# An attention and mixer kernel: halves of the first copies, the sixth pair's transposes, and the load of a small weight are moved

## The chip, the cores and the metric

The kernel runs on one core of a Trainium2 chip. The metric is device time in microseconds (us), the median of several executions. One more execution is profiled; its trace gives a start and a duration for every instruction. The engines are TensorE (PE for matmuls, PEld for its weight loads), VectorE (DVE), ScalarE (ACT), GpSimd (POOL) and SyncE (SP); a name with q is the queue of that engine from which it issues DMAs.

## What is computed

There are B = 8 batches of H = 8 heads, S = 576 tokens of D = 64 values, and 16 beacon keys and values ahead of the tokens. Causal attention gives x (8 x 576 x 512); a mixer of rank 32 along the tokens and a two-layer perceptron follow.

```
k_all = concat([beacon_k, k], axis=2); v_all = concat([beacon_v, v], axis=2)
scores = where(causal, -1e9, q @ k_all^T / sqrt(D))
a = softmax(scores)
x = (a @ v_all), heads side by side             # (B, S, 512)
u = x + (x^T @ U @ V)^T                         # U (576, 32), V (32, 576)
out = u + max(u @ w_ch1, 0) @ w_ch2             # w_ch1 (512, 2048), w_ch2 (2048, 512)
```

## The kernel before

**The tiles.** Attention runs by pairs of heads: a pair p is heads 2c and 2c + 1 of batch b, with b, c = divmod(p, 4), so pairs 0 to 3 are batch 0 and the sixth pair is p = 5. The layers run by blocks of 512 tokens over all batches. Banks of PSUM come from one ring of eight (`pst`), so the ninth tile waits until the first is read.

**One pair.** `qkT_units` (line 284) turns q and k: for each of the two, `one` makes 6 or 12 transposes on TensorE into one bank, and a copy moves them to qT or kT. For the first pair alone the copy is shared by ACT and DVE (line 623): `one` gives each half of the six token positions j, and as token 6p + j stands in column 6p + j, both halves write every column group. `score_units` (line 303) makes the products of keys and queries in four groups; visit 0 takes groups 0 and 1, visit 1 takes groups 2 and 3, or each alone ("two" and "three"). ACT's exponentials follow each visit; in pairs 0 to 4 the causal mask is added in PSUM by TensorE, in later ones DVE applies it to the exponentials. `av_unit` (line 353) makes a head's product with v, and DVE divides by the sum (lines 365 and 366) into xb.

**The mixing.** `mix_units` (line 370): `head` multiplies a batch's xb by Usb into qtp, which DVE copies to qts; `begin` and `most` add x, transposed by TensorE, and the product of qts with Vsb in four banks, which ACT and DVE in turn copy to uT ("settle", lines 402 to 408); `end` does so for the last 80 tokens with Vend, all on DVE.

**The layers.** `mlp_units` (line 442) gives 16 units `g_unit` (four matmuls with one 128-column slice of w1, then the rectifier on ACT or DVE) and 16 units `c_unit` (with w2). `feed` puts a block's units into a queue; `fill(n)` runs the next n. `FIRST` (line 653) says how many a slot p of the first eight runs between its attention steps. Block 0 needs uT of the first 512 tokens; its units 0 to 3 read w1's first quarter, 4 to 7 the second, and so on.

**The order.** All engines run what the program writes, in its order (line 699). In the first eight slots p (line 744), the steps of a slot are a list `seq`: the transposes of pair p + 2 (q, then k), a regroup of pair p + 3 from p = 4 on, visit 1 of the scores of pair p + 1, masks, the two products of pair p, and visit 0 of the scores of pair p + 2. Slot 3 is rewritten (line 767), as the first mixing is in it: products of pair 3, `cast_end`, transposes of pair 5, `head`, group two, `begin`, group three, `most`, `end`, visit 0 of pair 5. Four empty entries are then put ahead of block 0's units in the queue (line 780).

**The loads.** Most loads are issued by POOL, in order, each on one of a few semaphores, so a further load waits until an earlier one has landed. U and V are loaded by SP in `small_loads` (line 152) in float32: a marker that DVE writes holds the three loads of U and, behind them, the four copies of V until DVE has come that far. Then `cast` makes Usb and Vsb on POOL, and `cast_end` makes Vend on DVE. `load_rest` (line 731) calls them in slot 1 behind its second step; behind the cast, POOL issues the rest of v of batch 1, the last three quarters of w1, w2, and all later batches.

`keep_warm` (line 236) runs idle products of 512 columns on TensorE: eight at the start, two ahead of pair 0's scores, one ahead of pair 1's.

Of the kernel before, what the change touches and what calls it, by code (L numbers as in the profile page):

```python
# [11 lines left out]
F32 = mybir.dt.float32  # L12
# [6 lines left out]
P = 128  # L19
# [11 lines left out]
def kernel(  # L31
# [13 lines left out]
    nc = tc.nc  # L45
    B, H, S, D = q.shape
# [55 lines left out]
    def pst(shape, dtype, name):  # L102
        return psum.tile(shape, dtype, tag="ps", name=name)
# [48 lines left out]
    def small_loads():  # L152

        f = utp.tile([P, NT * R + S], F32, name="small", tag="ut")
        nc.vector.memset(f[:, 0:1], 0.0)
        uf, vf = f[:, 0 : NT * R].rearrange("p (j r) -> p j r", r=R), f[:, NT * R :]
        nc.sync.dma_start(out=uf[: nq[0], 0, :], in_=moe_U[0 : nq[0], :])
        nc.sync.dma_start(
            out=uf[:, 1 : NT - 1, :], in_=moe_U[q0[1] : QM, :].rearrange("(j p) r -> p j r", p=P)
        )  # L160
        nc.sync.dma_start(out=uf[:NL, NT - 1, :], in_=moe_U[QM:S, :])
        for cc in range(NCC):
            nc.sync.dma_start(out=vf[ds(R * cc, R), :], in_=moe_V)

        def cast():
            for rr, jj in ((nq[0], slice(0, 1)), (P, slice(1, NT - 1)), (NL, slice(NT - 1, NT))):
                nc.gpsimd.tensor_copy(out=Usb[:rr, jj, :], in_=uf[:rr, jj, :])
            nc.gpsimd.tensor_copy(out=Vsb, in_=vf[:, 0:QM])

        def cast_end():  # L170
            for cc in range(NCC):
                rs = ds(R * cc, R)
                nc.vector.tensor_copy(out=Vend[rs, cc, :], in_=vf[rs, QM:S])

        return cast, cast_end

    def emit_w1(i):
        w1r = moe_w_ch1.rearrange("(cc p) f -> p cc f", p=P)
# [105 lines left out]
    def qkT_units(turns, qT, kT, c, copies=((nc.vector.tensor_copy,), (nc.vector.tensor_copy,))):  # L284

        def one(i, dst, b0):
            ps = pst([P, SK], F16, name="tps")
            for j in range(TJ):
                n = TP + b0 if j == TJ - 1 else TP
                turns[i](ps, TP * j, n, j)  # L290
            w = TJ // len(copies[i])
            for a, copy in enumerate(copies[i]):
                js = slice(w * a, w * (a + 1))
                copy(  # L294
                    out=dst[:, c, b0 : b0 + S].rearrange("x (p j) -> x p j", j=TJ)[:, :, js],
                    in_=ps[:, 0:S].rearrange("x (j p) -> x p j", j=TJ)[:, :, js],
                )
            if b0:
                copies[i][-1](out=dst[:, c, 0:b0], in_=ps[:, S : S + b0])

        return [lambda: one(1, qT, 0), lambda: one(0, kT, Nb)]
# [348 lines left out]
    LAG = 10  # L650
    HINT = 5

    FIRST = [0, 0, 0, 0, 7, 5, 4, 4]

    QUOTA = {2: 4}

    IDLE = [8, 2, 1, 0]
    queue = []
    state = {"t": 0}

# [38 lines left out]
    with tc.manual_schedule(engines={ENG.PE, ENG.Activation, ENG.DVE, ENG.SP, ENG.Pool}):  # L699
        load_first()  # L700
        build_masks()
        for src, dst in zip((k[0], q[0]), Ls[0][0]):
            token_load(nc.gpsimd, src, dst, HALVES[1])
        v_beacon(beacon_v[0], vss[0])
        v_tokens(v[0], vss[0], HALVES[0])
        prs[0][0] = regroup(first, 0, 0, V, act_copy, beacons=False)
        keep_warm(pst([P, 512], F32, name="idle"), IDLE[0], plain)
        t0, sc = qkT_of(0), scores_of(0)
        for u in t0:
            u()  # L710
        sc[0](IDLE[1])
        masks = sc[2]
        prs[1] = [None, regroup(first, 1, 1, V)]
        for u in qkT_of(1)[::-1]:
            u()
        clear()
        sc[1]()
        sc = scores_of(1)
        sc[0](IDLE[2])

        Ls[1] = qk_tiles()
        (kt, qt), _ = Ls[1]
        token_load(nc.gpsimd, k[1], kt, HALVES[0])
        token_load(nc.gpsimd, q[1], qt, HALVES[0])
        key_beacons(nc.gpsimd, beacon_k[1], kt, ALLH)
        v_tokens(v[0], vss[0], HALVES[1])
        token_load(nc.gpsimd, k[1], kt, HALVES[1])
        token_load(nc.gpsimd, q[1], qt, HALVES[1])
        emit_w1(0)

        def load_rest():
            cast, cast_end = small_loads()
            cast()
            v_beacon(beacon_v[1], vss[1])
            v_tokens(v[1], vss[1], HALVES[0])
            emit_w1(1)
            v_tokens(v[1], vss[1], HALVES[1])
            emit_w1(2)
            emit_w1(3)
            emit_w2()  # L740
            return cast_end

        NP1 = NF * NH2
        for p in range(NP1):
            b, c = divmod(p, NH2)
            if c == 0 and NF <= b + 1:
                load_batch(b + 1)
            seq = []
            prior = masks
            if p + 2 < NP1:  # L750
                seq += [lambda i=i, p=p: qkT_of(p + 2)[i]() for i in range(2)]
            if NH2 + 3 <= p + 3 < NP1:
                seq.append(lambda p=p: regroup_of(p + 3))
            if p + 1 < NP1:
                one_by_one = sc[3]
                seq.append(sc[1])
                masks = sc[2]
            seq += [prior] + av_of(p)
            sc = []
            if p + 2 < NP1:  # L760
                new_qT_of(p + 2)
                sc = scores_of(p + 2)
                seq.append(lambda sc=sc, p=p: sc[0](IDLE[3] if p < NH2 else 0))
            if p == NH2 - 1:
                two, three = one_by_one
                _, head, (most, end), begin = mix_units(xbs[b], 0, False)
                seq = (
                    seq[-3:-1] + [cast_end] + seq[0:2] + [head, two, lambda: begin([0, 1]), three, most, end] + seq[-1:]
                )
            done = 0  # L770
            for i, u in enumerate(seq):
                u()
                if p == 1 and i == 1:
                    cast_end = load_rest()
                want = FIRST[p] * (i + 1) // len(seq)
                fill(want - done)
                done = want
            if c == NH2 - 1:
                if b == 0:
                    queue.extend([None] * 4)  # L780
                    feed(b)
                else:
                    mix(b)

        fill(AHEAD - 8)
        regroup_of(NP1)
        regroup_of(NP1 + 1)
        fill(8)
        t0, sc, t1 = qkT_of(NP1), scores_of(NP1), qkT_of(NP1 + 1)
        for u in t0 + sc[0:1] + t1[0:1] + sc[1:3] + t1[1:2]:  # L790
            u()
            fill(1)
        regroup_of(NP1 + 2)
        tr = []
        for p in range(NP1, NP):
            b, c = divmod(p, NH2)
            if c == 0 and b + 1 < B:
                load_batch(b + 1)
            if c == (2 if b + 2 == DT0 else 1) and DT0 <= b + 2 < B:
                load_whole(b + 2)  # L800
            if c == 0 and b + 1 == DT0:
                tr = turns(b + 1)
            if c == NH2 - 1 and DT0 < b + 2 < B:
                tr = turns(b + 2)
            sc = scores_of(p + 1) if p + 1 < NP else []
            qk = qkT_of(p + 2) if p + 2 < min(NP, DT0 * NH2) else []
            av = av_of(p)
            if c == NH2 - 1 or c == 0 and b + 1 == DT0:
                fill_turns(tr, NT)
            if c == 0 and b > NF:  # L810
                mix(b - 1)
            if c == (1 if b + 1 == DT0 else 0):
                fill_turns(tr, NT)
            seq = sc[0:1] + av[0:1] + qk[0:1] + sc[1:3] + qk[1:2] + av[1:2]
            if p + 3 < min(NP, DT0 * NH2):
                seq.append(lambda p=p: regroup_of(p + 3))
            quota = QUOTA.get(b, 9)
            done = 0
            for i, u in enumerate(seq):
                u()  # L820
                want = quota * (i + 1) // len(seq)
                fill(want - done)
                done = want
        mix(B - 1)
        guard()


        queue.insert(len(queue) - 22, guard_sum)
        fill(len(queue) - 12)
        n_bad = nc.values_load(badi[0:1, 0:1], min_val=0, max_val=P)  # L830
        fill(len(queue) - HINT)
        with tc.block():
            tc.mark_branch_hint_location("general", engines=[ENG.PE, ENG.Activation, ENG.DVE, ENG.SP, ENG.Pool])
            fill(len(queue))
# [95 lines left out]
```

## Time and profile before

| what | value |
|---|---|
| median of 3 runs | 360.03 us (359.12 to 363.38) |
| the profiled execution | 359.74 us |
| its span, first to last instruction | 358.1 us |
| mean granted TensorE clock | 0.990 |
| TensorE matmul busy | 350.0 us in 3134 instructions |
| VectorE busy | 188.5 us |
| ScalarE busy | 166.4 us |
| GpSimd busy | 96.3 us |

The views used are these. A row of the windows gives the stretch in us, its length, then the busy time of PE, PEld, DVE, ACT and POOL, each with its count of instructions, then the granted TensorE clock as a share of the full one, the busy share of the DMA engines, and GB/s. A row of the timeline gives the start in us, the duration in us, engine, line, operation, the tiles as out<-in, the shape and the count; in square brackets stands the idle time of the engine just before it and what ended it ("issue" where nothing that the profile shows ended it). A row of several instructions covers all of them, and its last matmul's tail overlaps what follows. A row of the chain of waits gives a start, a duration, and the work that the chain ran through; a DMA there lasts from its issue to its landing.

### The profile page before, as it was taken

How to read it: one execution, taken by the hardware profiler on the slowest of the kernel's cores; microseconds unless marked ns; L12 is line 12 of the kernel's file. 1: busy time of each engine (PE TensorE's matmuls, PEld its weight loads, DVE VectorE, ACT ScalarE, POOL GpSimd, SP SyncE). 2: the span in 40 equal slices, each digit the busy share in tenths (PEclk: the TensorE clock that was granted, in tenths of full speed). 3: DMA queues.
4: the chain of work that ended last, by engine and by line, in shares of the span. 5: the costliest groups of instructions: out<-in, count | busy, mean ns of one | idle time of the engine just before them, and what ended most of it. 6: DMA issues, size and time to landing. Idle time of an engine off the chain costs nothing.

```text
span 358.1 us, 7829 instructions
## 1 busy us (share of the span) xinstructions
PE 350.0 (98%) x3134; PEld 175.2 (49%) x3134; DVE 188.5 (53%) x488; ACT 166.4 (46%) x356; POOL 96.3 (27%) x135
## 2 busy tenths in 40 slices
PE   8989999999999999999999999999999999999995
PEld 3665455455565444444444444444454444444443
DVE  4667754588986454563455447445745522313311
ACT  4976761469646364367444654556503202401400
POOL 8729711609139027403730400000000000000000
PEclk9996999999999999999999999999999999999999
DMA  8998999999999949997999794142013215114111
GB/s 172 143 174 78 174 208 188 195 179 136 121 84 138 190 102 111 148 206 102 135 141 203 122 121 105 60 101 55 31 60 95 60 59 95 25 59 89 31 60 63
DMA packets 143946, 41.37 MB, mean 116 GB/s; under 512 B 128800, under 2 KB 139296, under 8 KB 143904
## 3 DMA queue, kind: packets, MB, share of 16 engines
q0 software_dynamic: 87408, 18.18, 67.4%
q1 hardware_dynamic: 56272, 22.34, 32.6%
q8 instruction: 26, 0.43, 0.5%
q10 hardware_dynamic: 224, 0.30, 0.2%
q14 instruction: 16, 0.13, 0.1%
HBM read 37.59 MB, written 9.44 MB: 131 GB/s over the span
## 4 chain that ended last, share of the span: by engine, by line
PE 81%; DMA 10%; DVE 3%; POOL 2%; SPq 1%; ACT 1%; issue 1%; ACTq 0%; POOLq 0%
PE cps L477 32%; PE gps L461 31%; PE sps L330 7%; PE po L357 6%; DMA st<-in_beacon_k_dram 6%; DMA w<-in_moe_w_ch_dram 2%; DMA small<-in_moe_V_dram 2%; PE tps L261 1%; DMA stk<-in_k_dram 1%; POOL vs L209 1%; PE cph L502 1%; ACT expt L336 1%; PE qtp L386 1%; DVE pr L254 1%; PE ups L422 1%; DVE uT L404 1%
## 5 line engine op out<-in xcount | busy, mean ns | idle before, releaser
L336 ACT ACTIVATE expt<-sps 128x496 f16<-128x496 f32 (+2 forms) x256 | 111.5, 532 | 63.0 <-PE sps L330 62.7
L461 PE MATMUL gps<-uT,w 128*128 128x512 f16 x576 | 135.5, 380 | 0.0
L477 PE MATMUL cps<-w,gT 128*128 128x512 f16 x560 | 132.7, 380 | 0.0
L465 ACT ACTIVATE gT<-gps 128x512 f16<-128x512 f32 x86 | 51.9, 607 | 95.8 <-PE gps L461 95.8
L461 PEld LDWEIGHTS <-w 128*128 128x128 f16 x576 | 52.1, 98 | 59.4 <-issue 3.4
L477 PEld LDWEIGHTS <-gT 128*128 128x128 f16 x560 | 49.8, 97 | 59.2 <-issue 6.8
L467 DVE TENSOR_SCALAR gT<-gps 128x512 f16<-128x512 f32 x58 | 40.0, 690 | 47.8 <-PE gps L461 46.7
L490 DVE TENSOR_TENSOR ob<-cps,ut 128x512 f32<-128x512 f32 x31 | 21.4, 690 | 49.6 <-PE cps L477 49.2
L357 PEld LDWEIGHTS <-expt 128*128 128x128 f16 (+1 forms) x960 | 36.8, 98 | 15.2 <-issue 1.9
L209 POOL DMA_DIRECT2D vs<-in_v_dram x50 | 39.5, 807 | 15.4 <-PE po L357 4.8
L357 PE MATMUL po<-vs,expt 128*128 128x65 f16 (+1 forms) x960 | 39.6, 195 | 0.2 <-DVE ob L490 0.2
L330 PE MATMUL sps<-qT,kT 64*128 64x80 f16 (+4 forms) x384 | 35.4, 290 | 0.1
L366 DVE TENSOR_TENSOR xb<-po,rec 128x320 f16<-128x320 f32 x64 | 31.5, 492 | 2.2
L307 DVE TENSOR_TENSOR expt<-expt,bigmask 128x512 f16<-128x512 f16 x54 | 22.6, 419 | 11.7 <-ACT expt L336 11.7
L365 DVE RECIPROCAL rec<-po 128x5 f32<-128x5 f32 x64 | 12.0, 187 | 23.2 <-PE po L357 23.2
L330 PEld LDWEIGHTS <-kT 64*128 64x128 f16 x384 | 11.8, 95 | 23.3 <-issue 15.3
L191 POOL DMA_DIRECT2D vs<-in_beacon_v_dram x8 | 4.3, 532 | 59.3 <-PE po L357 59.3
L560 POOL DMA_DIRECT2D st<-in_q_dram x20 | 16.9, 865 | 3.7 <-DMA vs<-in_v_dram 3.0
L560 POOL DMA_DIRECT2D st<-in_k_dram x20 | 16.9, 870 | 1.9 <-DMA vs<-in_v_dram 1.8
L404 DVE TENSOR_TENSOR uT<-ups,uT 128x496 f16<-128x496 f32 x20 | 12.1, 667 | 6.8 <-PE ups L422 3.6
L294 DVE COPY qT<-tps 128x576 f16<-128x576 f16 (+1 forms) x16 | 11.8, 736 | 5.1 <-PE tps L261 2.4
L294 DVE COPY kT<-tps 128x576 f16<-128x576 f16 (+1 forms) x16 | 11.7, 733 | 1.7 <-PE tps L267 1.1
(84 smaller groups left out, 145.6 us busy)
## 6 DMA issues: line engine op xcount, KB each, us to landing
out_dram<-ob SPq DMA_DIRECT2D x35, 256.0 KB, 2.2
vs<-in_v_dram POOLq DMA_DIRECT2D x18, 128.0 KB, 8.4
w<-in_moe_w_ch_dram POOLq DMA_DIRECT2D x4, 512.0 KB, 8.7
w<-in_moe_w_ch_dram POOLq DMA_DIRECT2D x2, 1024.0 KB, 14.5
st<-in_k_dram POOLq DMA_DIRECT2D x12, 128.0 KB, 7.4
st<-in_q_dram POOLq DMA_DIRECT2D x12, 128.0 KB, 9.3
st<-in_k_dram POOLq DMA_DIRECT2D x2, 576.0 KB, 13.1
st<-in_q_dram POOLq DMA_DIRECT2D x2, 576.0 KB, 16.1
```

The lines of the kernel that those rows point to most:

```text
L209: nc.gpsimd.dma_start(out=dst[a : a + nq[j], j, :, :], in_=src[hs, ds(q0[j], nq[j]), :].rearrange("h p d -> p h d"))
L294: copy(out=dst[:, c, b0 : b0 + S].rearrange("x (p j) -> x p j", j=TJ)[:, :, js], in_=ps[:, 0:S].rearrange("x (j p) -> x p j", j=TJ)[:, :, js],
L307: nc.vector.tensor_tensor(out=e4, in0=e4, in1=bigmask, op=ALU.min)
L330: nc.tensor.matmul(ps[g, i][:, ds(o, w)], kT[hp, c, ds(P * ch, P)], qT[hp, c, ds(qa, w)], start=not early, stop=True, skip_group_check=early,)
L336: nc.scalar.activation(out=ex[i][:, ds(SLOT * g, gw[g])], in_=ps[g, i][:, 0 : gw[g]], func=AF.Exp, scale=scale)
L357: nc.tensor.matmul(po[:, j, :], ex[0 : nk[c], ds(blk[(c, j)], P)], vs[0 : nk[c], ds(c * H * E + h * E, E)], start=(c == 0), stop=(c == j),)
L366: nc.vector.tensor_tensor(out=xb[:, :, ds(h * D, D)], in0=po[:, :, 0:D], in1=r.broadcast_to([P, NT, D]), op=ALU.mult)
L461: nc.tensor.matmul(g[:, 0:n], w1[:, cc, ts(dc, P)], uT[:, cc, ds(t0, n)], start=(cc == 0), stop=(cc == NCC - 1))
L465: nc.scalar.activation(out=gT["t"][:, dc, 0:n], in_=g[:, 0:n], func=AF.Relu)
L467: nc.vector.tensor_scalar_max(out=gT["t"][:, dc, 0:n], in0=g[:, 0:n], scalar1=0.0)
L477: nc.tensor.matmul(ps[:m, :], gT["t"][:, dc, ds(P * i, m)], w2[:, dc, :], start=(dc == 0), stop=turned and dc == NDC - 1, skip_group_check ...
L560: nc.gpsimd.dma_start(out=dst[a : m[j], j, :, :], in_=src[:, ds(q0[j], nq[j]), :].rearrange("h p d -> p h d"))
```

## The change

There are five edits.

1. In `qkT_units`, a copy that is shared is split by tokens: each engine takes half of the token groups p, with all six j, so it writes one half of the columns in a piece. Where one engine copies, nothing changes.
2. `small_loads` becomes a generator in three steps. U is loaded in slot 0 behind its second step (before: slot 1, second step). V, with a marker of its own, and the rest of `load_rest` follow at the end of slot 0.
3. Slot 3 is reordered: `head` and the mixing come right behind the products of pair 3, and the transposes of pair 5 behind `end`. Behind them block 0 is put into the queue and two of its units are run, and then comes visit 0 of pair 5. The four empty entries are gone.
4. `FIRST` for slots 4 to 7 goes from 7, 5, 4, 4 to 4, 4, 3, 3. With the two units of slot 3, and without the four empty entries, both kernels run 16 units of block 0 by the end of slot 7.
5. One idle product on a bank of its own is put between the transposes of q and of k of pair 0.

```
     def small_loads():
...
         nc.sync.dma_start(out=uf[:NL, NT - 1, :], in_=moe_U[QM:S, :])
+        yield
+        nc.vector.memset(vf[:, 0:1], 0.0)
         for cc in range(NCC):
             nc.sync.dma_start(out=vf[ds(R * cc, R), :], in_=moe_V)
...
-        return cast, cast_end
+        yield cast, cast_end
...
-            w = TJ // len(copies[i])
+            w = TP // len(copies[i])
             for a, copy in enumerate(copies[i]):
-                js = slice(w * a, w * (a + 1))
+                part = slice(w * a, w * (a + 1))
                 copy(
-                    out=dst[:, c, b0 : b0 + S].rearrange("x (p j) -> x p j", j=TJ)[:, :, js],
-                    in_=ps[:, 0:S].rearrange("x (j p) -> x p j", j=TJ)[:, :, js],
+                    out=dst[:, c, ds(b0 + TJ * w * a, TJ * w)].rearrange("x (p j) -> x p j", j=TJ),
+                    in_=ps[:, 0:S].rearrange("x (j p) -> x p j", j=TJ)[:, part, :],
                 )
...
-    FIRST = [0, 0, 0, 0, 7, 5, 4, 4]
+    FIRST = [0, 0, 0, 0, 4, 4, 3, 3]
...
-    IDLE = [8, 2, 1, 0]
+    IDLE = [8, 2, 1, 0, 1]
...
-        for u in t0:
-            u()
+        t0[0]()
+        keep_warm(pst([P, 512], F32, name="idle"), IDLE[4])
+        t0[1]()
...
         def load_rest():
-            cast, cast_end = small_loads()
+            cast, cast_end = next(loads)
             cast()
...
             if p == NH2 - 1:
...
+                def layers():
+                    feed(0)
+                    fill(2)
+
                 seq = (
-                    seq[-3:-1] + [cast_end] + seq[0:2] + [head, two, lambda: begin([0, 1]), three, most, end] + seq[-1:]
+                    seq[-3:-1] + [cast_end, head, two, lambda: begin([0, 1]), three, most, end]
+                    + seq[0:2] + [layers] + seq[-1:]
                 )
...
                 u()
-                if p == 1 and i == 1:
+                if p == 0 and i == 1:
+                    loads = small_loads()
+                    next(loads)
+                if p == 0 and i == len(seq) - 1:
                     cast_end = load_rest()
...
             if c == NH2 - 1:
-                if b == 0:
-                    queue.extend([None] * 4)
-                    feed(b)
-                else:
+                if b > 0:
                     mix(b)
```

## Prediction

> **What bounds the kernel now.** I read the page's busy times first, then windows of five microseconds and of one, then the timeline of the stretches that the change touches, and last the chain of waits for the landings of the loads.
>
> ```profile
> PE 350.0 (98%) x3134; PEld 175.2 (49%) x3134; DVE 188.5 (53%) x488; ACT 166.4 (46%) x356; POOL 96.3 (27%) x135
> ```
>
> ```profile
> 20.00:25.00 5.00, 3.92 (x97) 2.94 (x96) 3.48 (x11) 4.21 (x10) 0.67 (x3) 1.00 1.20 201
> 25.00:30.00 5.00, 4.22 (x65) 2.73 (x66) 2.67 (x9) 1.88 (x5) 3.22 (x6) 0.73 0.52 70
> 30.00:35.00 5.00, 5.00 (x66) 3.05 (x64) 4.36 (x11) 4.31 (x10) 5.00 (x8) 0.59 1.11 91
> 27.00:28.00 1.00, 0.29 (x3) 0.10 (x2) 1.00 (x2) 0.48 (x2) 1.00 (x3) 0.65 0.07 12
> ```
>
> TensorE is busy in 350.0 of 358.1 us, so 8.1 us is all that its idle time can give. Behind 35 us the windows show next to no gap, so a microsecond won ahead of it stays won unless a load is late. The stretch from 20 to 35 us is where this change works, and three things go wrong there at once. TensorE idles 1.08 + 0.78 us (windows one and two), its granted clock is 0.73 and 0.59 (half from about 27.3 on, since (0.27 + 0.41) x 5 / 0.5 = 6.8 us at half clock), and the DMA engines fall to a share of 0.07 at 27 us. The two idles are in these rows:
>
> ```profile
> 17.52 0.06 DVE L155 MEMSET small<- 128x1 f32 x1
> 18.98 2.56 SPq L163 DMA_DIRECT2D small<-in_moe_V_dram  x4
> 22.29 1.09 PE L357 MATMUL po<-vs,expt 128*128 128x65 f16 x30
> 23.81 0.49 DVE L366 TENSOR_TENSOR xb<-po,rec 128x320 f16<-128x320 f32 x1
> 25.00 0.32 PE L267 MATMUL tps<-ident,st 96*64 96x96 f16 x5 [1.08 <-issue]
> 25.25 0.47 PE L386 MATMUL qtp<-xb,Usb 112*32 112x128 f16 x20
> 25.65 0.36 PE L322 MATMUL sps<-negmask,identb 128*128 128x128 bf16 x4
> 26.26 0.61 PE L397 MATMUL ups<-ident,xb 112*128 112x112 f16 x8
> 26.71 0.22 PE L322 MATMUL sps<-negmask,identb 128*128 128x128 bf16 x1
> 26.80 0.60 POOL L168 CAST Vsb<-small 128x496 f16<-128x496 f32 x1 [1.78 <-DMA small<-in_moe_V_dram]
> 27.71 0.26 PE L322 MATMUL sps<-negmask,identb 128*128 128x128 bf16 x1 [0.78 <-DVE qT L294]
> 28.20 1.01 PE L397 MATMUL ups<-ident,xb 112*128 112x112 f16 x8
> 29.79 1.26 DVE L406 CAST uT<-ups 128x496 f16<-128x496 f32 x2 [1.20 <-PE ups L422]
> 30.31 0.98 PE L330 MATMUL sps<-qT,kT 64*128 64x496 f16 x4
> 30.96 0.48 DVE L406 CAST uT<-uend 128x320 f16<-128x320 f32 x1
> ```
>
> V is issued on SP from 18.98 us, and its last part holds the cast of Vsb on POOL until 26.80; the casts of Vend on DVE wait for the same parts. Behind Vend, in DVE's order, wait the copies of the sixth pair, whose bank the 0.78 us stall waits for; behind Vsb, in POOL's order, wait all later loads. The 1.08 us stall carries no releaser.
>
> **The change, part by part.** *U and V sooner.* V's start moves from behind the DVE work of slot 1 to behind that of slot 0, whose last product is here:
>
> ```profile
> 15.36 0.49 DVE L366 TENSOR_TENSOR xb<-po,rec 128x320 f16<-128x320 f32 x1
> 20.48 6.17 DMA small<-in_moe_V_dram
> 31.42 7.25 DMA w<-in_moe_w_ch_dram
> 39.56 1.04 PE L461 MATMUL gps<-uT,w 128*128 128x512 f16 x4
> ```
>
> The product ends at 15.85; one more marker (0.06, on an idle DVE) lets SP issue V at 15.93 in place of 18.98, 3.05 us sooner. U goes out after slot 0's copies, ahead of V, so it no longer delays V by its three issues. No compute waits behind SP's queue here. POOL's order does not change: it stands at the cast anyway, and everything behind the cast moves with V. Thus the second quarter of w1, which lands at 31.42 + 7.25 = 38.67, should land at about 35.6. Bounds for this shift: 0 if V only queues longer behind the loads of batches 0 and 1, and 4.0 if its 6.17 us also shrink by a microsecond in a shorter queue. I take 3.05, because every later load follows V's issue and the empty DMA stretch at 27 us can take them.
>
> [...]
>
> *Slot 3 reordered.* TensorE reaches the head of the first mixing right behind the two attention products (22.29 + 1.09 = 23.38), so the 24 transposes no longer cover DVE's last product, which ends at 23.81 + 0.49 = 24.30: a new wait of about 0.85 us, in place of the 1.08 and the 0.78. Behind it, at full clock: head 0.40 (25.25 to 25.65), group two 0.61 (to 26.26), first half of the mixing 0.45 (to 26.71), group three about 0.3, and 2.11 us of half-clock work (28.20 to 30.31), about 1.05 at full clock. That ends at 27.1. The 24 transposes take 0.64 (15.59 to 16.23 below), with a 0.2 us wait for a bank of the mixing that ACT empties: 27.95.
>
> ```profile
> 11.55 0.58 PE L330 MATMUL sps<-qT,kT 64*128 64x496 f16 x4
> 15.59 0.71 PE L267 MATMUL tps<-ident,st 96*64 96x96 f16 x24
> 16.23 0.63 PE L322 MATMUL sps<-negmask,identb 128*128 128x128 bf16 x6
> 31.23 1.18 PE L267 MATMUL tps<-ident,st 96*64 96x96 f16 x24
> 80.41 0.87 PE gps L461 x4
> 77.99 0.46 PE po L357 x15
> 39.15 0.48 PE L330 MATMUL sps<-qT,kT 64*128 64x336 f16 x8
> 37.66 0.69 PE L261 MATMUL tps<-ident,pr 96*128 96x96 f16 x12
> ```
>
> *Two layer units ahead of the scores.* The first unit reads all of uT, so it waits for DVE's settling, 1.26 + 0.48 = 1.74 us from about 26.95: it starts at 28.7, a wait of 0.75. Two units of 0.87 end at 30.45 and cover the copies to qT and kT, which DVE finishes at about 30.3. The scores (0.5) end at 31.0, where before they ended at 31.23 with no unit done. If that cover were gone, the scores would wait 1.6 us for the copies.
>
> From 31.0 the new order is transposes 0.64, unit 0.87, scores 0.41 (39.15 to the unit at 39.56), unit 0.87, product 0.46, with about 0.4 of waiting for ACT's exponentials: the fifth unit is reached at 34.65. It is the first that reads w1's second quarter, so it waits until 35.6: a new stall of 0.95 (bounds: 0, and 4.0 if the quarter lands at 38.67 as before). Before, that unit stood at 39.56, 0.9 us behind its quarter. To be where the kernel before was at 39.56, the new order still owes a product 0.46, scores 0.51 (0.58 without the tail of 0.07), transposes 0.55 (0.69 without a tail of 0.14) and scores 0.41, together 1.93: it is there at 35.65 + 1.93 = 37.6, a gain of 1.95.
>
> *The new quota (4, 4, 3, 3).* The same 16 units are run before slot 8 in both. In slots 6 and 7 one unit less stands between attention steps, and one instead of two (1.73 us) between the last product and the next head. That head needs DVE's 0.19 + 0.49 us; one unit of 0.87 just covers it. Bounds 0 to 0.5; I take 0.2 lost.
>
> *First copies by tokens, and the idle product.*
>
> ```profile
> 5.92 0.48 DVE L294 COPY qT<-tps 128x288 f16<-128x288 f16 x1 [0.39 <-ACT qT L597]
> 5.59 0.66 PE L261 MATMUL tps<-ident,pr 96*128 96x96 f16 x6 [0.32 <-DVE pr L254]
> 6.33 1.03 PE L241 MATMUL sps<-ident 128*128 128x512 f16 x2
> 6.97 0.48 DVE L294 COPY kT<-tps 128x288 f16<-128x288 f16 x1 [0.57 <-ACT kT L597]
> 7.69 0.98 PE L330 MATMUL sps<-qT,kT 64*128 64x496 f16 x4
> 10.77 13.44 ACT L336 ACTIVATE expt<-sps 128x496 f16<-128x496 f32 x32 [0.49 <-PE sps L330]
> ```
>
> DVE's half waits 0.39 and 0.57 us for ACT's half, since interleaved halves span the same bytes; halves by tokens do not. The keys are whole 0.5 us sooner, but TensorE reaches its scores only 0.1 us before now, held by its idle and mask products. The idle product (0.43 to 0.5) fits in the 0.32 us wait, so it costs 0.1 at most; it could end the slow start sooner (0.98 at 7.69 against 0.58 at 11.55 for the same four products). Together -0.1 to 0.6. What they win reaches slot 3 only through the gapless run of 32 exponentials up to 24.21, and by then the slots also wait for tokens that POOL loads, which do not move. I take 0.
>
> **The sum.** 1.95 - 0.2 = 1.75 us. The profiled execution took 359.74 (span 358.1), 0.29 under the median of the runs, 360.03. 359.74 - 1.75 = 357.99, so 358.0. The next load that could take the gain back is batch 2's, due at 42.82 + 20.49 = 63.31 with transposes at 64.32:
>
> ```profile
> 42.82 20.49 DMA st<-in_beacon_k_dram
> 64.32 0.42 PE L261 MATMUL tps<-ident,pr 96*128 96x96 f16 x6
> ```
>
> It moves with V, by 3.05, so 1.75 passes; if it moved by less than about 1.5, it would be late next.
>
> **The rivals.** *The weights are not sooner (slower).* If w1's second quarter lands at 38.67 as before, the fifth unit starts at 38.7 and the state of 39.56 is reached at 40.65: 1.1 us lost and the quota's 0.2, so 361.0. It decides from a landing at 37.4, a shift under 1.3 us. For it: the DMA share of 1.20 while V is under way. Against: the DMA engines are nearly empty at 27 us. Chance 0.13.
>
> *The clock is halved again.* TensorE idles 0.85 and 0.75 us in the same stretch, less than 1.08 + 0.78 but not by much. With half clock from 27.3 for the 6.8 us of before, two units take 3.46, scores 0.98 and transposes 1.18: 34.3 us from 28.7; then 2.6 at full clock to the fifth unit, 36.9, which no longer waits; state at 38.85, gain 0.7 less 0.2: 359.2. Chance 0.16. [...]
>
> *The weights are in time.* If the quarter lands by 34.65, the 0.95 us stall is gone: 357.0. It needs V to land a microsecond faster than 6.17. For it: V then no longer contends with w1's first quarter. Against: no row shows a shorter queue at 16 us. Chance 0.18.
>
> **Chances.** Forecast (357.3 to 358.8) 0.49, weights in time 0.18, clock 0.16, weights late 0.13, anything else 0.04. From 356.0 to 360.8 lie the forecast, the clock, most of the early weights with up to a microsecond more, and rather over half of the late ones, so about 0.88. The forecast's own range is 357.3 to 358.8. All cases lie inside 2% of 360.03 (352.8 to 367.2), which is about what a measurement of this kernel tells from no change: faster 0.02, same 0.96, slower 0.02.
>
> **What would show it.** In the changed profile: V issued near 16 us and the Vsb cast near 23.7; no DVE wait on ACT at the first copies; the head waiting for DVE's product; the first unit at about 28.7 and behind it the scores without a wait; the fifth unit behind a wait for a DMA near 35.6; a granted clock of 1.00 from 25 to 35 us. I am wrong if the Vsb cast is not two microseconds sooner, if a clock under 0.8 remains, or if a wait over half a microsecond appears behind 40 us.

## The result, and the profile after

The changed kernel took 358.49 us in the median of 22 runs, the kernel before 360.39 in 22 runs beside them. The ratio is 0.9948, with a 95% interval of 0.9929 to 0.9968: 1.9 us faster, well inside 2%.

The execution profiled with that result fell in a slower state that some executions show (363.27 us), so the profile after is that of another execution of the same kernel, `full_again`, which took 359.49 us with a span of 357.7. That is 1.0 us above the median, and why is told below. First the page's busy times, then its windows; the columns are as before.

```profile
PE 347.8 (97%) x3135; PEld 174.2 (49%) x3135; DVE 188.8 (53%) x489; ACT 165.9 (46%) x356; POOL 96.3 (27%) x135
```

```profile
20.00:25.00 5.00, 3.66 (x52) 2.32 (x52) 2.15 (x7) 2.64 (x8) 2.21 (x5) 0.76 1.32 207
25.00:30.00 5.00, 4.34 (x86) 3.33 (x84) 2.52 (x9) 3.00 (x8) 5.00 (x8) 0.90 1.31 102
30.00:35.00 5.00, 4.17 (x69) 2.31 (x69) 4.00 (x8) 2.30 (x5) 4.33 (x7) 1.00 1.61 165
```

The DMA engines no longer run empty (1.31 in the second row, 0.52 before). The half clock (0.50 in the window from 28 to 29 us before) is shorter and has moved ahead: (0.24 + 0.10) x 5 / 0.5 = 3.4 us, where it was 6.8. But the first window now has more idle time than before: TensorE is busy 3.66 us there, not 3.92. The timeline of `full_again` names what stands in it:

```profile
13.44 0.31 SPq L157 DMA_DIRECT2D small<-in_moe_U_dram  x1
15.76 1.71 SPq L165 DMA_DIRECT2D small<-in_moe_V_dram  x4
20.72 0.47 POOL L169 CAST Usb<-small 128x96 f16<-128x96 f32 x2 [0.90 <-DMA small<-in_moe_U_dram]
21.87 0.31 PE L359 MATMUL po<-vs,expt 128*128 128x65 f16 x5 [1.03 <-DMA vs<-in_v_dram]
22.50 0.99 PE L359 MATMUL po<-vs,expt 80*128 80x65 f16 x16 [0.32 <-DMA vs<-in_v_dram]
23.26 0.60 POOL L170 CAST Vsb<-small 128x496 f16<-128x496 f32 x1 [2.08 <-DMA small<-in_moe_V_dram]
27.20 0.44 PE L388 MATMUL qtp<-xb,Usb 112*32 112x128 f16 x17 [0.66 <-DVE xb L368]
31.83 1.89 PE L463 MATMUL gps<-uT,w 128*128 128x512 f16 x8 [0.82 <-DVE uT L408]
33.65 0.58 PE L332 MATMUL sps<-qT,kT 64*128 64x496 f16 x4
37.52 1.03 PE L463 MATMUL gps<-uT,w 128*128 128x512 f16 x4
51.84 0.63 PE L359 MATMUL po<-vs,expt 128*128 128x65 f16 x15 [0.25 <-DVE expt L309]
```

U and V are where the edit put them, and the two waits that the prediction placed in slot 3 are there (0.66 and 0.82). The scores behind the two units (33.65) and the fifth unit (37.52) wait for nothing. New is a wait for v, 1.03 + 0.32 us, with the half clock behind it. The chain of waits, and the view of the tile w for the one load of w1's second quarter, give the two landings that matter:

```profile
15.74 6.71 DMA vs<-in_v_dram
```

```profile
L182 POOL DMA_DIRECT2D w<-in_moe_w_ch_dram x1: 774/774/774, 27.9 to 27.9; - x1
...
DMA to landing us min/median/max: 6.0/6.0/6.0
```

The last tokens of batch 0's v land at 15.74 + 6.71 = 22.45. The quarter of w1 lands at 27.9 + 6.0 = 33.9, 4.8 us sooner than the 38.67 of before.

Where the time is decided can be read off one place, the head of the second mixing. From the tile view of qtp (first and last start at the end), before and `full_again`:

```profile
L386 PE MATMUL qtp<-xb,Usb x20: 217/220/231, 54.1 to 54.3; 128*32 128x128 f16 x12, 112*32 112x128 f16 x4, 80*32 80x128 f16 x4
```

```profile
L388 PE MATMUL qtp<-xb,Usb x20: 216/220/230, 54.6 to 54.8; 128*32 128x128 f16 x12, 112*32 112x128 f16 x4, 80*32 80x128 f16 x4
```

In this one execution the changed kernel is not ahead at all. Behind this place the profiles of all kernels here take 303.1 to 305.1 us more, without an order between the kernels, so it decides the time to within a microsecond or so. What differs between the two spans is busy time: TensorE is busy 347.8 us in place of 350.0, and idle for 9.9 us in place of 8.1. So the runs have to say what is typical. Of the 44 compared executions of the changed kernel, 30 had a mean clock of 0.997 or more, so none of them can hold a whole stretch like this one (3.4 us at half clock take 0.5 x 3.4 / 358 = 0.005 off the mean); their median is 358.06 us. The other 14 lie between 358.97 and 362.55. Of 90 compared executions of the kernel before, 7 kept the clock (median 359.55). `full_again`, at 0.994, is one of the 14.

### The profile page after: what moved, and what is told of

It is laid out like the page before. It is cut to its first block, busy times and chain, and to the rows that moved or that the text cites. A ratio compares the mean times of both kernels' runs of the same rounds, so it can differ in the third digit from the quotient of the medians.

```text
span 361.6 us, 7837 instructions
## 1 busy us (share of the span) xinstructions
PE 350.1 (97%) x3135; PEld 175.3 (48%) x3135; DVE 188.2 (52%) x489; ACT 166.0 (46%) x356; POOL 96.4 (27%) x135
## 4 chain that ended last, share of the span: by engine, by line
PE 84%; DMA 8%; DVE 2%; POOL 2%; SPq 2%; issue 1%; POOLq 0%; DVEq 0%
PE gps L463 34%; PE cps L479 32%; PE po L359 7%; PE sps L332 6%; DMA uT<-xb 3%; DMA small<-in_moe_V_dram 2%; DMA st<-in_q_dram 2%; DMA vs<-in_v_dram 1%; PE tps L263 1%; SPq L379 1%; POOL vs L211 1%; PE cph L504 1%; PE qtp L388 1%; DVE uT L406 1%; PE ups L424 1%
## 5 line engine op out<-in xcount | busy, mean ns | idle before, releaser
L359 PEld LDWEIGHTS <-expt 128*128 128x128 f16 (+1 forms) x960 | 37.8, 99 | 18.8 <-issue 4.5
L359 PE MATMUL po<-vs,expt 128*128 128x65 f16 (+1 forms) x960 | 40.8, 196 | 3.1 <-DMA vs<-in_v_dram 2.7
L309 DVE TENSOR_TENSOR expt<-expt,bigmask 128x512 f16<-128x512 f16 x54 | 22.6, 418 | 11.7 <-ACT expt L338 11.7
L332 PEld LDWEIGHTS <-kT 64*128 64x128 f16 x384 | 11.9, 95 | 23.8 <-issue 16.7
```

What stands on the lines that cost most here:

```text
L309: nc.vector.tensor_tensor(out=e4, in0=e4, in1=bigmask, op=ALU.min)
L332: nc.tensor.matmul(ps[g, i][:, ds(o, w)], kT[hp, c, ds(P * ch, P)], qT[hp, c, ds(qa, w)], start=not early, stop=True, skip_group_check=early,)
L359: nc.tensor.matmul(po[:, j, :], ex[0 : nk[c], ds(blk[(c, j)], P)], vs[0 : nk[c], ds(c * H * E + h * E, E)], start=(c == 0), stop=(c == j),)
```

## The experiments

Ratios are to the kernel before, run beside each kernel on the same chip, with 95% intervals.

**`loads_only`**: before with the second edit alone.

```diff
+        yield
+        nc.vector.memset(vf[:, 0:1], 0.0)
...
-            cast, cast_end = small_loads()
+            cast, cast_end = next(loads)
...
-                if p == 1 and i == 1:
+                if p == 0 and i == 1:
+                    loads = small_loads()
+                    next(loads)
+                if p == 0 and i == len(seq) - 1:
                     cast_end = load_rest()
```

> Edit 2 alone: U in slot 0 behind its second step, V and the rest of the loads at the end of slot 0; slot 3, the quota, the first copies and the idle product as before. Theory A (the gain comes from the loads, the new order only uses them): the casts of Vend no longer hold DVE, the 0.78 us stall and the half clock behind it go, and the second quarter of w1 lands near 35.6 instead of 38.67; 1 to 2.5 us faster. Theory B (the gain comes from the new order of slot 3 with its two layer units): within 0.5 us of before. Theory C (U and V push the loads of batch 0 back): a wait of TensorE for v of batch 0 near 20 us, and no gain or a loss.

357.55 us, 0.9915 (0.988 to 0.9951): the loads alone bring more than the whole change. The timeline of `loads_only`:

```profile
22.49 0.92 PE L359 MATMUL po<-vs,expt 128*128 128x65 f16 x21 [1.21 <-DMA vs<-in_v_dram]
26.14 0.44 PE L388 MATMUL qtp<-xb,Usb 112*32 112x128 f16 x17 [0.16 <-DVE xb L368]
28.21 0.22 PE L324 MATMUL sps<-negmask,identb 128*128 128x128 bf16 x1 [0.42 <-DVE qT L296]
```

The wait for v is here too, so it belongs to the loads and not to the order. The old order then waits 0.16 + 0.42 where the new one waits 0.66 + 0.82.

TensorE is busy in 346.4 of 355.9 us in this profile, so it idles for 9.5 us, more than the 8.1 of before: in these two executions the gain is the half clock that did not come. The clock is not all of it. The old order with the new loads (this run, and `no_order` and `no_order_again` below) kept its clock, by the same 0.997, in 19 of 24 executions, with a median of 357.25; the 7 of the kernel before that kept it have 359.55, its other 83 have 360.81. Why a kept clock gave the kernel before so little is argued and not shown: its fifth unit stood only 0.9 us behind its quarter of w1, where a faster TensorE would have waited.

**`order_only`**: before with the third and fourth edits (the new slot 3 and the quota), the loads left where they were.

```diff
-    FIRST = [0, 0, 0, 0, 7, 5, 4, 4]
+    FIRST = [0, 0, 0, 0, 4, 4, 3, 3]
...
-                    seq[-3:-1] + [cast_end] + seq[0:2] + [head, two, lambda: begin([0, 1]), three, most, end] + seq[-1:]
+                    seq[-3:-1] + [cast_end, head, two, lambda: begin([0, 1]), three, most, end]
+                    + seq[0:2] + [layers] + seq[-1:]
```

> Edits 3 and 4 alone: slot 3 reordered with two layer units ahead of the scores, and the new quota; U and V are loaded as late as before. Theory A: the head waits for Usb and the mixing for Vend and Vsb (26.8 us), the fifth unit waits for w1's second quarter at about 38.7; 0.5 to 2 us slower than before. Theory B: 1 to 2 us faster.

361.95 us, 1.0032 (1.0007 to 1.0057). Its timeline has the first rival at its very place:

```profile
38.89 1.89 PE L461 MATMUL gps<-uT,w 128*128 128x512 f16 x4 [3.12 <-DMA w<-in_moe_w_ch_dram]
```

The fifth unit waits 3.12 us for w1, until 38.89. Without the sooner loads the new order is a loss. The price holds for the late w1 alone, and is not that of the order with the new loads.

**`first_only`**: before with the first and fifth edits (halves by tokens, the idle product).

```diff
-            w = TJ // len(copies[i])
+            w = TP // len(copies[i])
...
-    IDLE = [8, 2, 1, 0]
+    IDLE = [8, 2, 1, 0, 1]
```

> Edits 1 and 5 alone: the first copies halved by tokens and the idle product. Theory A: the first exponential some 0.1 to 0.6 us sooner, but slot 3 starts no sooner, so within 0.3 us of before. Rival: the sooner start goes through, 0.5 us or more faster.

360.89 us, 0.9991 (0.9968 to 1.0014): nothing, as costed. Its timeline shows something else, since the loads are the old ones here:

```profile
26.25 0.35 PE L386 MATMUL qtp<-xb,Usb 128*32 128x128 f16 x12 [2.21 <-POOL Usb L167]
```

The head waits 2.21 us for POOL's cast of U. In the kernel before, this place had 1.08 us under "issue", without a releaser. Its own timeline has the last part of that cast, which waits for U's landing, ending at 24.81 + 0.21 = 25.02, close to where TensorE went on (25.00):

```profile
24.81 0.21 POOL L167 CAST Usb<-small 80x32 f16<-80x32 f32 x1 [1.84 <-DMA small<-in_moe_U_dram]
```

**`full_again`**: the changed kernel once more, beside the three above.

> The changed kernel once more, for a profile without the wait of 2.41 us for v of batch 0. Theory A: 1.5 to 2 us faster, the clock full from 10 us on, a wait at the fifth unit for w1 near 35.6. Theory C: the wait for v of batch 0 near 20 us is there in every profile, shorter, 0.3 us or more.

359.35 us, 0.9944 (0.9917 to 0.9972). Parts and whole agree in sign: loads -3.3 us, order +1.1, first copies 0 give -2.2; the whole gave -1.5.

**`no_order`**: the changed kernel with the old slot 3 and quota (the two blocks of `order_only`, undone).

```diff
-                    seq[-3:-1] + [cast_end, head, two, lambda: begin([0, 1]), three, most, end]
-                    + seq[0:2] + [layers] + seq[-1:]
+                    seq[-3:-1] + [cast_end] + seq[0:2] + [head, two, lambda: begin([0, 1]), three, most, end] + seq[-1:]
```

> The changed kernel with edits 3 and 4 undone: loads, first copies and idle product as changed; slot 3 and the quota as before. Theory D (with V sooner, the new order of slot 3 costs more than it gives, since it trades the 24 transposes' cover for a wait for DVE's last product and one for uT): 2.5 to 3.5 us faster than before, so about 1 us faster than the changed kernel. Theory A as predicted (the two units ahead are worth about 1.7 us): slower than the changed kernel by a microsecond.

357.37 us, 0.9921 (0.989 to 0.9951). With the loads in place, undoing the order did not slow the kernel.

**`no_layers`**: the changed kernel without the two units ahead of the scores, with the old quota and the four empty entries of before.

```diff
-                    + seq[0:2] + [layers] + seq[-1:]
+                    + seq[0:2] + seq[-1:]
```

> The changed kernel without the two layer units ahead of the scores, with the quota and the empty entries of before; slot 3 otherwise as changed. As predicted: the scores wait about 1.6 us for the copies of the sixth pair, so 0.5 to 1.5 us slower than the changed kernel. Rival: the wait is paid back, since the first unit no longer waits 0.8 us for uT and later units have their turn anyway; within 0.5 us of it.

361.05 us, 1.0001 (0.9969 to 1.0033): the whole gain is gone. Its timeline and its window:

```profile
30.45 0.83 PE L332 MATMUL sps<-qT,kT 64*128 64x496 f16 x4 [2.14 <-DVE kT L301]
```

```profile
30.00:35.00 5.00, 4.55 (x61) 2.88 (x62) 3.32 (x10) 3.49 (x8) 3.99 (x7) 0.66 1.57 161
```

The scores wait 2.14 us for DVE's copies, and the clock halves behind that ((0.34 x 5) / 0.5 = 3.4 us in this window). So the two units do cover the copies, as the change needs them to.

**`u_only`**: before with U's loads alone moved to slot 0; V stays in slot 1, with a marker of its own.

```diff
+                if p == 0 and i == 1:
+                    loads = small_loads()
+                    next(loads)
                 if p == 1 and i == 1:
```

> The kernel before with U alone in slot 0; V and the rest stay in slot 1, though V now follows its own marker and not the three issues of U. Theory A (V's landing is what counts, and it comes about 1.3 us sooner): 0.3 to 1.3 us faster, v of batch 0 in time or late by under 0.5 us. Theory C with U as the culprit (576 rows of 128 bytes): a wait for v of batch 0 near 20 us of about 1 us, as in the changed kernel.

358.58 us, 0.9937 (0.9912 to 0.9962): 1.75 us, where both loads gave 2.96 in `no_order` beside it. This is not U alone. With U's three issues gone from ahead of it, V is issued from 16.94 us in this profile, 2.0 us sooner than before, and w1's quarter at 28.7, where it was 31.4. The wait for v is small in its timeline:

```profile
20.84 0.98 PE L359 MATMUL po<-vs,expt 128*128 128x65 f16 x21 [0.33 <-DMA vs<-in_v_dram]
24.54 0.44 PE L388 MATMUL qtp<-xb,Usb 112*32 112x128 f16 x17 [0.16 <-DVE xb L368]
```

**`v0_first`**: the changed kernel, with the second half of batch 0's v issued by POOL ahead of the keys and queries of batch 1.

```diff
+        v_tokens(v[0], vss[0], HALVES[1])
         token_load(nc.gpsimd, k[1], kt, HALVES[0])
...
         key_beacons(nc.gpsimd, beacon_k[1], kt, ALLH)
-        v_tokens(v[0], vss[0], HALVES[1])
```

> The changed kernel with one move on POOL: the second half of v of batch 0 is issued ahead of k, q and beacons of batch 1 and no longer behind them. Theory C (the 1.3 us wait for v of batch 0 is the price of the early U and V): the wait goes, 1 to 1.5 us faster than the changed kernel. Rival: k and q of batch 1 come late in its place and the transposes of pair 4 near 18 us wait; within 0.5 us of the changed kernel.

362.15 us, 1.0048 (1.0019 to 1.0077). The wait does not go, it changes its tile:

```profile
22.42 1.11 PE L269 MATMUL tps<-ident,st 96*64 96x96 f16 x24 [2.15 <-DMA st<-in_q_dram]
```

The transposes of batch 1's queries now wait 2.15 us. In this run the place of one load in POOL's order only decided which tile waits.

**`no_uv`**: the changed kernel with the loads of U and V left out.

```diff
-        nc.vector.memset(f[:, 0:1], 0.0)
+        nc.vector.memset(f, 0.0)
...
-        for cc in range(NCC):
-            nc.sync.dma_start(out=vf[ds(R * cc, R), :], in_=moe_V)
```

> The changed kernel with the loads of U and V left out (a cleared tile is cast in their place, so the mixing adds nothing). Theory C (U and V, put ahead, delay v of batch 0): no wait for v of batch 0 near 20 us, its last landing at about 18 to 19 us, POOL's cast free at once, and 1.5 to 3 us faster than the changed kernel. Rival (the wait has another cause, such as the queue of POOL itself): a wait of 1 us or more stays.

357.66 us, 0.9924 (0.9896 to 0.9951). The waits of TensorE over 0.3 us between 20 and 35 us in its timeline, and its first window:

```profile
23.40 0.44 PE L381 MATMUL qtp<-xb,Usb 112*32 112x128 f16 x17 [0.80 <-DVE xb L361]
28.04 1.89 PE L456 MATMUL gps<-uT,w 128*128 128x512 f16 x8 [0.83 <-DVE uT L401]
```

```profile
20.00:25.00 5.00, 4.20 (x101) 3.14 (x97) 3.76 (x13) 3.71 (x9) 4.62 (x7) 1.00 1.25 169
```

The wait for v and the half clock are gone, and only the two waits of the new order are left. This profile is of the fastest of its eight executions, so the other profiles have to bear it out. From the view of the tile vs, POOL's loads of v between 13 and 18 us in `no_uv` and then in `full_again`:

```profile
L204 POOL DMA_DIRECT2D vs<-in_v_dram x4: 677/761/770, 12.9 to 15.1; - x4
DMA to landing us min/median/max: 4.7/5.0/5.3
```

```profile
L211 POOL DMA_DIRECT2D vs<-in_v_dram x5: 669/752/760, 12.8 to 15.7; - x5
DMA to landing us min/median/max: 5.7/6.0/6.8
```

They are issued at much the same time, and take longer to land in `full_again`. The slowest of batch 0's loads of v takes 5.3 us in `no_uv`, 5.5 in `order_only`, 5.8 in `two_banks` and 6.3 before, and in none of these profiles, nor in that of `first_only`, does TensorE wait for v of batch 0 behind 20 us. With early U and V and v's place as it was, the slowest takes 6.6 us in `no_layers`, 6.8 in `full_again`, 7.0 in `no_order_again`, 7.3 in `loads_only` and 8.1 in the execution of 363.27 us, and 4.3 in `no_order`. In five of these six and `full_third`, seven in all, TensorE waits 1.2 us or more; `no_order` and `no_layers` have no such wait. So the early loads of U and V are what made v late here, though not in every execution.

**`two_banks`**: before, with the transposes of each half of a shared copy in a PSUM tile of its own; the halves stay interleaved.

```diff
-            ps = pst([P, SK], F16, name="tps")
+            m = len(copies[i])
+            w = TJ // m
+            pss = [pst([P, SK], F16, name="tps") for _ in range(m)]
...
-                    in_=ps[:, 0:S].rearrange("x (j p) -> x p j", j=TJ)[:, :, js],
+                    in_=pss[a][:, 0 : TP * w].rearrange("x (j p) -> x p j", j=w),
```

> The kernel before with one change: where ACT and DVE share a copy, the transposes of positions 0 to 2 and 3 to 5 go to a bank each; the halves written stay interleaved. Theory E (DVE waits for ACT since both read one bank's tile): DVE's wait of 0.39 and 0.57 us is gone. Rival (it waits since both write interleaved columns of one tile): the wait stays. The time within 0.3 us of before in both cases.

360.71 us, 0.9995 (0.9975 to 1.0015). The first copies of DVE in the timeline of `full_again`, and then in that of `two_banks`:

```profile
5.75 0.46 DVE L296 COPY qT<-tps 128x288 f16<-128x288 f16 x1 [0.30 <-ACT qT L599]
6.54 0.46 DVE L296 COPY kT<-tps 128x288 f16<-128x288 f16 x1 [0.34 <-ACT kT L599]
```

```profile
5.64 0.47 DVE L295 COPY qT<-tps 128x288 f16<-128x288 f16 x1
6.37 0.48 DVE L295 COPY kT<-tps 128x288 f16<-128x288 f16 x1 [0.26 <-PE tps L278]
```

With halves by tokens, DVE still waits for ACT (0.30 and 0.34 us). With a bank for each half it does not, though the halves are written as interleaved as before, when it waited 0.39 and 0.57. What made DVE wait here is that both read one tile, which here is one bank; the run does not part the tile from the bank.

**`no_order_again`** and **`full_third`**: the kernels of `no_order` and of the change once more, side by side.

> The changed kernel with edits 3 and 4 undone, once more beside the changed kernel. Theory D (the new order of slot 3 costs its two waits, 0.66 and 0.82 us in the profile): 2.5 to 3.3 us faster than before and 1 to 1.5 us faster than the changed kernel. Rival: no difference between them, 0.3 us or less.

> The changed kernel once more, beside the one with edits 3 and 4 undone. Theory D: 1.5 to 2 us faster than before, with waits of about 0.66 at the head and 0.82 at the first unit. Theory C: the wait for v of batch 0 differs from profile to profile, 0 to 2.5 us.

357.59 us, 0.9906 (0.9877 to 0.9936), against 358.97, 0.9948 (0.9919 to 0.9977). The intervals overlap (0.9919 to 0.9936), but both times that old and new order stood side by side with the new loads, the old order was ahead: `loads_only` 0.9915 beside `full_again` 0.9944 (which differ in the first copies too, put at nothing by `first_only`), and this pair. `no_order` with 0.9921 agrees. The new order costs about 1.4 us here. Not all of that is the clock: among the executions that kept it, the median is 358.06 with the new order and 357.25 with the old. The waits differ by about as much, 0.66 + 0.82 in place of 0.16 + 0.42. The timeline of `no_order_again`:

```profile
21.77 0.31 PE L359 MATMUL po<-vs,expt 128*128 128x65 f16 x5 [0.72 <-DMA vs<-in_v_dram]
22.59 0.65 PE L359 MATMUL po<-vs,expt 80*128 80x65 f16 x16 [0.51 <-DMA vs<-in_v_dram]
25.96 0.44 PE L388 MATMUL qtp<-xb,Usb 112*32 112x128 f16 x17 [0.16 <-DVE xb L368]
```

It waits 1.23 us for v and keeps a clock of 1.00; `full_again` waited 1.35 and lost half its clock for 3.4 us.

## Why the prediction was right, and where it was not

The time was right: 358.0 forecast, 358.49 measured, a gain of 1.75 against 1.9. The direction and the sooner loads behind it were understood; that the size fits is in part luck. The sum holds one step that failed, one size that was too small, and one cause that it did not see, and their effects on the time run in opposite directions: w1 came sooner than forecast and v later, the loads were worth more and the new order took some of it back.

**The step that failed** is the last sentence on the first copies, that the slots wait for "tokens that POOL loads, which do not move". Their landings move, because U and V now travel beside them: those loads of v take 5.7 to 6.8 us to land in `full_again` and 4.7 to 5.3 in `no_uv`. v of batch 0 lands at 22.45 in `full_again`, and TensorE waits for it. Five of seven profiles with early U and V have such a wait, none of the five without, `no_uv` among them; in `v0_first` the lateness passes on to another tile (2.15 us). The prediction let V queue behind the loads of batches 0 and 1 in its lower bound for w1, and did not ask what V would cost those loads: 1.35 us of waiting for v in this trace.

**The fifth unit's stall of 0.95 us** did not come, for two reasons that both belong to the loads. The quarter of w1 was mis-sized: it moved by 4.8 us, not 3.05, beyond the bound of 4.0. V's cast, and with it the issue of w1, came 26.80 - 23.26 = 3.5 us sooner, and the quarter itself took 6.0 us in place of 7.25. And in `full_again` TensorE came to that unit late, at 37.52 and not 34.65. Of these 2.9 us, 1.35 are the wait for v, and up to 3.4 / 2 = 1.7 the half clock behind it.

**The weights-not-sooner rival** is real, and it is `order_only`: 361.95 against its 361.0. What kept it from happening is the shift of w1, with 3.5 us to spare over the 37.4 from which it decides (37.4 - 33.9).

**The clock.** The forecast of 1.00 from 25 to 35 us failed in `full_again` (0.90 up to 30, and 0.76 from 20 to 25, so the prediction's sign of a clock under 0.8 is there); it held in `loads_only` and `no_uv`, and 30 of 44 executions of the changed kernel have no whole stretch of half clock. Of the 14 others two were profiled, `full_again` and `full_third`, and in both the second rival happened, but at the wait for v and not at the two waits of slot 3 that it named. In `no_uv` these stand alone, 0.80 and 0.83 us with the 24 transposes between them, and the clock stays at 1.00. In `full_again` it fell behind 1.35 us of idle time in two pieces, and in `no_order_again` it did not fall behind 1.23. The stretch of half clock took 3.4 us in `full_again` and 6.8 in the kernel before. What parts 1.35 from 1.23 is not shown.

**The new order.** Both waits were right in place and nearly in size: 0.66 in `full_again` and 0.80 in `no_uv` for 0.85, 0.82 for 0.75. The cover of the two units was right in kind and too low in size: without them the scores wait 2.14 us, not 1.6. From the first unit to the head of the second mixing `full_again` takes 54.6 - 31.8 = 22.8 us. The prediction's own numbers give 22.6 without the stall: 34.65 - 28.7 to the fifth unit, 1.93 to the old state, 54.1 - 39.56 from there, and 0.2 for the quota. The two parts are off by more, with opposite signs: 5.7 us to the fifth unit in place of 5.95, and 17.1 from there in place of 16.7. A wait of 0.25 stands at 51.84, which is near the quota's 0.2, though no run takes the quota alone. What the sum did not do was price the old order with the new loads. It wrote the whole 1.95 us down to the change as one state, and so it could not see that the loads alone are worth 3.3 us and that the order gives some of it back, 1.4 in the last pair and 1.8 between `loads_only` and `full_again`.

**The stall of 1.08 us** was quoted without a releaser and left at that. In `first_only` the wait at this place names U's cast (2.21 us), and before, the stall ended within 0.02 us of that cast. `two_banks`, with the old loads too, waits 1.60 us for the same cast. That U's landing was the cause in the kernel before is argued from this and not shown: its own row names nothing, and what went on at 25.00 were the last five transposes, which do not read U. `u_only` does not settle it, as V moved with U there.

**The first copies** were rightly costed at nothing, and the reason was wrong. Halves by tokens do wait (0.30 and 0.34 us); `two_banks`, in which DVE no longer waits for ACT, shows that the shared tile and its bank decided here, not the columns. The wait is worth no time that these runs can show. Nor is a sooner end of the slow start: the first four score products take 0.58 us in `full_again` and 0.98 before, and `first_only` gained nothing (0.9991). No run takes the idle product alone.

**What stays open.** No execution of the changed kernel that kept its clock was profiled: `full_again` and `full_third` show the wait for v and a stretch of half clock (mean clocks of 0.994 and 0.992), while 30 of 44 executions had no such stretch. That those wait less for v is likely and not shown. Nor is it known why the wait is 0 in the profile of `no_order` and 1.23 in that of `no_order_again`, the same kernel.

## What to carry to other kernels

Run the parts of a change alone: here one part was worth 3.3 us and another took over one back, and the sum had priced neither alone. When a load is moved ahead, name every load in flight beside it and the engine that is waiting for that one; here V's issue 3.2 us sooner went with 1.35 us of waiting for v in `full_again`. A stall without a releaser should be held against every cast and landing that ends at its end, before it is left out of the argument.

## What the hardware showed

- Two small weights issued 4.2 us (U) and 3.2 us (V) sooner by SP delayed loads that POOL had issued: those of v took 5.7 to 6.8 us to land in `full_again` and 4.7 to 5.3 in `no_uv`, where U and V are not loaded, and TensorE waited 1.35 us for them in the first. With the late load moved ahead on POOL (`v0_first`), TensorE waited 2.15 us for queries of batch 1.
- Behind 1.35 us of idle time in `full_again` and 2.14 in `no_layers` the clock stood at half for 3.4 us; behind 1.23 in `no_order_again` it stayed at 1.00. An estimate from the 3.4 us is that such a stretch is worth up to 1.7 us on top of the stall. 30 of 44 executions of the changed kernel had none.
